# Attention, MLP and routed experts in one kernel: r*k by (d, t) for tiles 3 to 6, lower halves on VectorE, reciprocals by a backward scan

## The chip, the cores and the metric

One core of a Trainium2 chip runs the whole program. The metric is the device time of one execution in microseconds (us). Within the core, TensorE (PE) multiplies matrices out of SBUF into PSUM, VectorE (DVE) and ScalarE (ACT) work elementwise on SBUF and PSUM, GpSimd (POOL) works elementwise on SBUF, and SyncE (SP) issues the DMA transfers. Every engine takes its instructions strictly in the order of its own queue.

## What is computed

Three stages follow one another: a linear attention with a decaying state, an MLP with a leaky activation, and a top-1 mixture of experts.

```python
# attention: B 4, H 8, S 768, D 48
for t in range(S):
    cur = einsum('bhd,bhe->bhde', u[None] * k_t, v_t)
    y[:, :, t] = einsum('bhd,bhde->bhe', r_t, state + cur)
    state = w_t[:, :, :, None] * state + einsum('bhd,bhe->bhde', k_t, v_t)
# MLP: 3072 tokens, 384 -> 2048 -> 384
h = x @ w_in
x = (where(h > 0, h, alpha * h)) @ w_out
# experts: 8 experts, 384 -> 1024 -> 384, one per token
e = argmax(x @ w_gate);  g = softmax(x @ w_gate)[e]
out = g * (relu(x @ w1[e]) @ w2[e])
```

## The kernel before

**Tiles and blocks.** The 3072 tokens are 24 tiles of 128 (`NTILE`); a batch has six (`CPB`), so tiles 0 and 6 begin a sequence (`first`) and tile 5 ends one (`last`). Three tiles make a block of the MLP (`NB`), and there are 8 blocks. The attention of the three tiles of block b+1 is interleaved with the MLP steps of block b. Tiles 0 to 2 have nothing to hide under; they, and the first weights, make up the prologue (slots from `PT0`).

**One attention tile** (`att_tile`). `dm` holds r, k and w with the head dimension on partitions and time along the row, (d, t); `tm` holds r, k and v with time on partitions. `scan` makes the running product of w on DVE (`ex`); POOL multiplies r by it (`decay_r`); `rec` forms its reciprocal on DVE, with one reciprocal of every fourth column (112x128) and three products that fill the columns between (L310); then k is multiplied by the reciprocal (L312). `diag` and `diag_sum` form the diagonal term: POOL multiplies r by k and by u on `tm` (L317, L318), DVE sums over d (`c`, L323), and `diag_v` multiplies v by c on POOL (`cv`). PE makes the scores, ACT copies them out, POOL masks them (`at`, L362), and PE accumulates the output from cv, the state and the masked scores in one bank (`px`). `state` adds the old state to k^T v on DVE and multiplies by the decay `pm` on POOL (L396, L397). `x_out` and `x_low` split the output into a high half on ACT (`xth`) and a low half on DVE (`xtl`, L440).

**Weights.** w_in and w_out come as 64-bit numbers in 16 loads (`wl_dma`, `wl_stages`): per load ACT rescales, DVE does three passes of integer work (L212, L213, L216), ACT rounds the high half, and the low half is one subtraction of 128x768 (L234). The even loads (w_in, `wil`) have it on DVE, the odd ones (w_out, `wol`) on POOL; `LOW_V` says which. Two raw buffers and two `v64` buffers are in use, so a load waits for the words of the one two before it.

**MLP step.** A step is nine matmuls of 128x384 (`p1`), ACT and DVE for the activation (`gn`, then `gt` on DVE), ACT and DVE for its two halves (`gh`, then `gl` on DVE), and, two steps later, nine matmuls of 128x384 (`p2`). After a block, `p2_out` copies three banks of PSUM to `x2`, one of the three on DVE. `gate_block` then routes the block's tokens: in blocks 0 to 5 DVE forms the logits with 24 products that sum (`lv`, L483); in the last two blocks PE does it, with three transposes and three small matmuls per tile (`tr`, `lg`).

**Order.** Slots in a table (`OPS`, `PRO_OPS`, `PRO_MOVED`, times `s_tile`) set where a piece of work is issued. In the prologue all engines keep that order. From the first MLP step on, PE and POOL keep it, and the order on DVE and ACT is chosen by the framework's scheduler.

Of the kernel before, what the change touches and what calls it, by code (L numbers as in the profile page):

```python
# [64 lines left out]
LOW_V = range(0, 16, 2)  # L65
# [6 lines left out]
}  # L72
PT0 = -100
# [28 lines left out]
def attention_mlp_moe(ctx, tc, dmaj, tmaj, ub, alpha, w_in, w_out, w_gate, w_gate_b, wexp, out):  # L102
# [59 lines left out]
    ub_s = cst.tile([128, DM], F32, name="ub_s")  # L162
    al_s = cst.tile([128, NF1], F32, name="al_s")
# [36 lines left out]
    def wl_stages(j):  # L200
# [47 lines left out]

    def constants():
# [20 lines left out]
    def att_tile(i, s0):  # L270
        cx = {}
        blk, j = divmod(i, NB)
        first, last = i % CPB == 0, i % CPB == CPB - 1
# [25 lines left out]
        def rec(n):  # L299
# [5 lines left out]
            if n == 0:  # L305
                vec.reciprocal(out=at4(rc, 3), in_=at4(ex, 3))
            elif n == 1:
                w = dm_t[i][:, 1024:1540].rearrange("p (a t) -> p a t", a=NP)[:, :, 1:129]
                for m in (2, 1, 0):
                    vec.tensor_tensor(out=at4(rc, m), in0=at4(rc, m + 1), in1=at4(w, m + 1), op=ALU.mult)  # L310
            else:
                vec.tensor_tensor(out=cx["k"], in0=cx["k"], in1=rc, op=ALU.mult)  # L312

        def diag():
            tm = tm_t[i]
            rk = ap.tile([128, DM], F32, tag="rk", name="rk", bufs=1)
# [55 lines left out]
        def ktr():  # L372
            pa = ps_a.tile([128, NP, PR], F32, tag="pa", name="pk")
            for p in range(NP):
                pe.transpose(pa[:, p, :], cx["k"][:, p, :], ident[:PR, :PR])
            cx["pk"] = pa

        def ktr_out():
            kt = ap.tile([128, NP, PR], F32, tag="kt", name="kt", bufs=1)
            act.copy(kt, cx["pk"])  # L380
            cx["kt"] = kt

        def kv():
            v = cx["v"]
            pa = y_bank("pv", [PR, NP, 96])
            for p in range(NP):
                pe.matmul(pa[:, p, :], lhsT=cx["kt"][:, p, :], rhs=v[:, 96 * p : 96 * p + 96], start=True, stop=True)
# [49 lines left out]
        def x_low():  # L437
# [5 lines left out]
            "scan": scan, "r": decay_r, "rec0": lambda: rec(0), "rec1": lambda: rec(1), "k": lambda: rec(2),  # L443
            "rk": diag, "c": diag_sum, "cv": diag_v, "sc": scores,
# [3 lines left out]
        if not last:  # L448
            ops.update({"ktr": ktr, "ko": ktr_out, "pm": decay, "kv": kv, "st": state})
        for n, fn in ops.items():  # L450
            if i < NB or (i == NB and n in PRO_NEXT):
                at_slot(PT0 + PRO_MOVED.get((i, n), PTILE * i + PRO_OPS[n]), fn)
            else:
                at_slot(s0 + OPS[n], fn)

    def gate_block(blk, x2, g0):
# [98 lines left out]
        if blk < NBLK - PE_GATES:  # L555
# [545 lines left out]
```

## Time and profile before

| | |
|---|---|
| three runs, median | 864.56 us (861.56 to 866.51) |
| the profiled execution | 865.85 us, of which the span is 864.2 us |
| PE busy | 806.4 us (93%) |
| DVE busy | 639.0 us (74%) |
| ACT busy | 380.1 us (44%) |
| POOL busy | 305.5 us (35%) |
| mean granted TensorE clock | 0.970 |

An engine is busy while one of its instructions executes; an instruction that has begun but is held up counts as busy too, so a long one of a kind that is elsewhere short tells of a hold-up. Idle time in front of an instruction is put down to what ended it (its releaser). The granted clock is 1.00 at 2.4 GHz and 0.50 at 1.2 GHz.

### The profile page before, as it was taken

Reading aid. Unit: us, or ns where it says so; the run is one execution under the profiler, and the core shown is the slowest. Engines: PE = TensorE matmul, PEld = TensorE weight load, DVE = VectorE, ACT = ScalarE, POOL = GpSimd, SP = SyncE. Lnnn points to the kernel's source line nnn. Section 1 sums busy time; section 2 is a strip of 40 time slices with the busy share of each in tenths; the row PEclk is TensorE's granted clock in tenths of the full one; section 3 lists DMA queues with packets and bytes.
Section 4 is the critical chain, followed back from the end, with each engine's and each line's share of the span. In section 5 each row is a group of like instructions: output and inputs, shape, how many; then the busy total and the mean of one; then the engine's idle time right before and its main releaser. Section 6 shows DMA issues by size and latency. Waiting matters only on the chain. (4 is left out here: it accounts for less than half of the span.)

```text
span 864.2 us, 15692 instructions
## 1 busy us (share of the span) xinstructions
PE 806.4 (93%) x5997; PEld 757.0 (88%) x5997; DVE 639.0 (74%) x1195; ACT 380.1 (44%) x727; POOL 305.5 (35%) x338
## 2 busy tenths in 40 slices
PE   5678888999999999999999999999999999999994
PEld 3577768999889989989999989989899999999993
DVE  5999997967967986975986973446776676766761
ACT  1445452344333334333344333346455666565641
POOL 5776625324443234243334331122333122222201
PEclk8889889999999999999999999999999999999998
DMA  9825543022223222322322300155367577686820
GB/s 270 249 89 201 182 146 126 35 66 94 67 66 97 65 66 66 94 66 71 90 66 67 93 1 2 29 201 211 119 229 246 198 235 289 221 286 200 289 104 20
DMA packets 30517, 114.80 MB, mean 133 GB/s; under 512 B 8229, under 2 KB 11592, under 8 KB 30440
## 3 DMA queue, kind: packets, MB, share of 16 engines
q1 hardware_dynamic: 26088, 103.52, 37.5%
q0 software_dynamic: 4352, 10.26, 3.2%
q8 instruction: 48, 0.79, 0.4%
q14 instruction: 29, 0.24, 0.1%
HBM read 104.10 MB, written 10.45 MB: 133 GB/s over the span
## 5 line engine op out<-in xcount | busy, mean ns | idle before, releaser
L582 PE MATMUL ph<-xth,wih 128*128 128x384 f32 x384 | 137.8, 359 | 16.4 <-DVE gt L587 13.5
L582 PE MATMUL ph<-xtl,wih 128*128 128x384 f32 x384 | 131.7, 343 | 7.2 <-DVE xtl L440 7.2
L608 PE MATMUL py<-woh,gh 128*128 128x384 f32 x384 | 135.6, 353 | 2.7 <-DVE x L619 2.4
L582 PE MATMUL ph<-xth,wil 128*128 128x384 f32 x384 | 132.3, 345 | 4.6 <-DVE wil L234 4.6
L593 ACT CAST gh<-gt 128x384 fp32r<-128x384 f32 x128 | 65.7, 513 | 151.0 <-DVE gt L587 150.4
L608 PE MATMUL py<-woh,gl 128*128 128x384 f32 x384 | 129.9, 338 | 0.0
L608 PE MATMUL py<-wol,gh 128*128 128x384 f32 x384 | 129.5, 337 | 0.0
L587 DVE SCALAR_TENSOR_TENSOR gt<-gn,oma_s,ph 128x384 f32<-128x384 f32 x128 | 77.6, 606 | 51.8 <-ACT gn L585 51.6
L595 DVE TENSOR_TENSOR gl<-gt,gh 128x384 fp32r<-128x384 f32 x128 | 87.8, 686 | 28.7 <-ACT gh L593 26.3
L483 DVE SCALAR_TENSOR_TENSOR sink<-x,wgb 128x384 f32<-128x384 f32 x144 | 100.0, 718 | 1.5 <-ACT x L619 1.2
L585 ACT ACTIVATE gn<-ph 128x384 f32<-128x384 f32 x128 | 62.4, 488 | 85.3 <-PE ph L582 82.1
L813 DVE SCALAR_TENSOR_TENSOR gl<-ph,gh 128x256 fp32r<-128x256 f32 x96 | 40.3, 421 | 74.7 <-ACT gh L811 74.4
L582 PEld LDWEIGHTS ph<-xth,wih 128*128 128x128 f32 x384 | 74.0, 193 | 24.1 <-DVE gt L587 16.7
L882 POOL DMA_INDIRECT out<-ys,meta x28 | 28.3, 1012 | 165.2 <-ACT ys L879 109.9
L808 PE MATMUL ph<-xh,w1h 128*128 128x256 f32 x288 | 81.7, 284 | 1.4 <-DVE gl L813 1.3
L608 PEld LDWEIGHTS py<-woh,gh 128*128 128x128 f32 x384 | 73.1, 190 | 9.7 <-issue 3.2
L808 PE MATMUL ph<-xh,w1l 128*128 128x256 f32 x288 | 81.2, 282 | 0.0
L582 PEld LDWEIGHTS ph<-xtl,wih 128*128 128x128 f32 x384 | 74.5, 194 | 7.5 <-DVE xtl L440 7.5
L808 PE MATMUL ph<-xl,w1h 128*128 128x256 f32 x288 | 80.7, 280 | 0.0
L582 PEld LDWEIGHTS ph<-xth,wil 128*128 128x128 f32 x384 | 74.2, 193 | 6.7 <-DVE wil L234 6.7
L362 POOL TENSOR_SCALAR_AFFINE_SELECT at<-at 128x512 f32<-128x512 f32 x46 | 34.2, 764 | 125.6 <-ACT at L358 125.6
L608 PEld LDWEIGHTS py<-woh,gl 128*128 128x128 f32 x384 | 72.8, 190 | 0.6 <-DVE gl L595 0.6
(213 smaller groups left out, 1874.0 us busy)
## 6 DMA issues: line engine op xcount, KB each, us to landing
raw<-w SPq DMA_DIRECT2D x64, 768.0 KB, 4.8
tm<-tmaj SPq DMA_DIRECT2D x21, 704.0 KB, 4.2
dm<-dmaj SPq DMA_DIRECT2D x21, 673.8 KB, 4.8
raw<-w_out SPq DMA_DIRECT2D x8, 768.0 KB, 4.3
raw<-w_in SPq DMA_DIRECT2D x7, 768.0 KB, 5.1
x2d<-x SPq DMA_DIRECT2D x8, 576.0 KB, 4.5
both<-tmaj SPq DMA_DIRECT2D x3, 704.0 KB, 11.1
wgb<-w_gate_b SPq DMA_DIRECT2D x2, 768.0 KB
```

The source lines that it names most:

```text
L362: pool.affine_select(out=cx[jj], in_=cx[jj], pattern=[[0, NP], [1, 128]], compare_op=ALU.is_gt, fill=0.0, base=0, channel_multiplier=-1,)
L483: vec.scalar_tensor_tensor(out=sink, in0=x2[:, j, :], scalar=1.0, in1=wgb_t[h][:, e, :], op0=ALU.mult, op1=ALU.mult, accum_out=cx["l"][:, ...
L582: pe.matmul(ph, lhsT=w, rhs=x[:, c, :], start=k == 0, stop=k == 3 * KC - 1)
L585: act.activation(gn, ph, AF.Relu, scale=-1.0)
L587: vec.scalar_tensor_tensor(out=gt, in0=gn, scalar=oma_s[:, f : f + 1], in1=ph, op0=ALU.mult, op1=ALU.add)
L593: act.copy(gh, gt)
L595: vec.tensor_tensor(out=gl, in0=gt, in1=gh.bitcast(F32), op=ALU.subtract)
L608: pe.matmul(y_t[blk][j], lhsT=g[:, sl], rhs=w, start=f == 0 and m == 0, stop=f == NF1 - 1 and m == 2,)
L808: pe.matmul(ph, lhsT=w, rhs=x, start=k == 0, stop=k == 3 * KC - 1)
L813: vec.scalar_tensor_tensor(out=gl, in0=ph, scalar=0.0, in1=gh.bitcast(F32), op0=ALU.max, op1=ALU.subtract)
L882: pool.indirect_dma_start(out=out, out_offset=bass.IndirectOffsetOnAxis(ap=d["meta"][:, j, 0:1], axis=0), in_=ys, in_offset=None, bounds_c ...
```

## The change

- `NBACK = 7`: for tiles 0 to 6 the reciprocals come from one reciprocal of four columns (112x4, the last of each pair of heads) put into a zeroed tile `inj`, and one scan of 516 columns that runs backward over w. `dm` gets one more column for it (`DMW` 1541 instead of 1540).
- `CPE`, tiles 3 to 6: POOL multiplies r by k in `dm`, once, 112x512; PE forms the sums with u, four matmuls of two columns behind the transposes of k; ACT copies them out with k^T. The second product on POOL and the sum on DVE are gone, the loads of r and k by time are cut away, and `cv` stands three slots later.
- `NSPE = 7`: for tiles 1 to 4 PE adds the old state by one matmul with the identity, and DVE multiplies by the decay out of PSUM. The product on POOL is gone.
- All 16 lower halves of the weights are on DVE.
- The routing of block 0 takes its logits from PE (`0 < blk` in `gate_block`). The constants of the routing are made at slot 34, after block 0, and `1 - alpha` is made on DVE.

```diff
-LOW_V = range(0, 16, 2)
+NSPE = 7
+NBACK = 7
+DMW = 2 * 512 + NP * 129 + 1
+CPE = range(NB, 7)
+OPS_C = {"rk": -10, "cv": 3}
...
-    (3, "scan"): 19.55, (3, "rec0"): 19.58, (3, "rec1"): 21.52, (3, "k"): 21.54,
+    (3, "rk"): 19.5, (3, "scan"): 19.55, (3, "rec0"): 19.58, (3, "rec1"): 21.52, (3, "k"): 21.54,
...
-        sp.dma_start(out=tm, in_=tmaj[i])
+        sl = (slice(None), slice(2 * DM if i in CPE else 0, TMW))
+        sp.dma_start(out=tm[sl], in_=tmaj[i][sl])
...
+    inj = ap.tile([PR, NP, 129], F32, tag="inj", name="inj", bufs=1)
+    pool.memset(inj, 0.0)
...
-            e = vec if j in LOW_V else pool
-            e.tensor_tensor(out=lo, in0=v, in1=hi.bitcast(F32), op=ALU.subtract)
+            vec.tensor_tensor(out=lo, in0=v, in1=hi.bitcast(F32), op=ALU.subtract)
...
-            if n == 0:
+            if n == 0 and i < NBACK:
+                vec.reciprocal(out=inj[:, :, 128], in_=ex[:, :, 127])
+                vec.tensor_tensor_scan(
+                    out=rc.rearrange("p a t -> p (a t)")[:, ::-1],
+                    data0=dm_t[i][:, 1025 : 1025 + NP * 129][:, ::-1],
+                    data1=inj.rearrange("p a t -> p (a t)")[:, ::-1],
+                    initial=0.0,
+                    op0=ALU.mult,
+                    op1=ALU.add,
+                )
...
+            if i in CPE:
+                rk = ap.tile([PR, NP, 128], F32, tag="rk", name="rk", bufs=1)
+                pool.tensor_tensor(out=rk, in0=cx["r"], in1=cx["k"], op=ALU.mult)
+                cx["rk"] = rk
+                return
...
+            if i in CPE:
+                for p in range(NP):
+                    at = NP * PR + 2 * p
+                    pe.matmul(pa[:, at : at + 2], lhsT=cx["rk"][:, p, :], rhs=us_s[:, p, :], start=True, stop=True)
...
+            add = not first and i < NSPE
+            if add:
+                fl = "p a e -> p (a e)"
+                pe.matmul(
+                    pa.rearrange(fl), lhsT=ident[:PR, :PR], rhs=st_t[i - 1].rearrange(fl), start=True, stop=False
+                )
...
-            if first:
+            if first or i < NSPE:
                 vec.tensor_tensor(out=sn, in0=pa, in1=pm, op=ALU.mult)
...
-        if blk < NBLK - PE_GATES:
+        if 0 < blk < NBLK - PE_GATES:
```

The POOL queue in block 0, from the mask of tile 3's scores to the mask of tile 4's. Before (`dm` is r by the decay, `st` the state, `wol` a lower half, `rk` and `cv` the diagonal term):

```order
L362 AFFINE_SELECT at_550<-at_550 128x512
L234 TENSOR_TENSOR wol_123<-v_503,woh_122 128x768
L297 TENSOR_TENSOR dm<-dm,ex 112x512
L397 TENSOR_TENSOR st<-st,pm 112x384
L317 TENSOR_TENSOR rk<-tm 128x384
L318 TENSOR_TENSOR rk<-rk,ub_s 128x384
L234 TENSOR_TENSOR wol_123<-v_594,woh_122 128x768
L234 TENSOR_TENSOR wol_123<-v_718,woh_122 128x768
L330 TENSOR_TENSOR cv<-tm,c 128x256
L330 TENSOR_TENSOR cv<-tm,c 128x128
L362 AFFINE_SELECT at_833<-at_833 128x512
```

The same place after, with the products of tiles 4 and 5 (`rk<-dm`):

```order
L398 AFFINE_SELECT at_539<-at_539 128x512
L349 TENSOR_TENSOR rk<-dm 112x512
L315 TENSOR_TENSOR dm<-dm,ex 112x512
L366 TENSOR_TENSOR cv<-tm,kt 128x256
L366 TENSOR_TENSOR cv<-tm,kt 128x128
L398 AFFINE_SELECT at_823<-at_823 128x512
```

The three lower halves, the state and the product with u have left this stretch; tile 3's cv, which stood ahead of its masks, now stands behind them and behind the two products of tile 4.

The DVE queue where block 0 ends (`c` is the sum of tile 7's diagonal term, COPY is the copy of a finished bank). Before:

```order
L312 TENSOR_TENSOR dm<-dm,rec 112x512
L587 SCALAR_TENSOR_TENSOR gt<-gn,oma_s,ph 128x384
L323 TENSOR_REDUCE c<-rk 128x8
L619 COPY x_1351<-py_601 128x384
L595 TENSOR_TENSOR gl<-gt,gh 128x384
L483 SCALAR_TENSOR_TENSOR sink,lg<-x_1351,wgb 128x384 x4
```

And after:

```order
L342 TENSOR_TENSOR dm<-dm,rec 112x512
L641 SCALAR_TENSOR_TENSOR gt<-gn,oma_s,ph 128x384
L673 COPY x_1345<-py_590 128x384
L649 TENSOR_TENSOR gl<-gt,gh 128x384
L359 TENSOR_REDUCE c<-rk 128x8
```

The copy of the bank now stands ahead of the sum `c`, and the products of the routing that followed are gone from here.

## Rows read from the trace of the kernel before

**Rows 1.** Waits of TensorE, 43.68 to 130 us: total, times, longest (us)
```profile
PE ph L582 <- DVE xtl L440: 7.2, 1, 7.2
PE ph L582 <- DVE gt L587: 6.9, 2, 4.2
PE ph L582 <- DVE wil L234: 4.6, 4, 1.6
```

**Rows 2.** Busy time by stretch, with the granted clock in third place from the end
```profile
26.30:43.70 17.40, 9.95 (x145) 6.99 (x143) 17.13 (x20) 6.92 (x14) 12.45 (x11) 0.89 0.77 239
43.68:130.00 86.32, 70.48 (x474) 61.78 (x475) 84.44 (x105) 43.67 (x80) 50.28 (x41) 0.86 0.47 155
...
146.00:226.00 80.00, 79.76 (x625) 74.46 (x626) 65.45 (x160) 29.36 (x68) 27.59 (x34) 0.98 0.26 78
```

**Rows 3.** DVE in order of time at the end of the prologue: start, duration (us)
```profile
30.54 3.68 DVE L282 TENSOR_TENSOR_SCAN ex<-dm,apat 112x516 f32<-112x516 f32 x1
34.26 0.96 DVE L306 RECIPROCAL rec<-ex 112x128 f32<-112x128 f32 x1
35.13 0.49 DVE L212 TENSOR_SCALAR v<-v 128x768 uint32<-128x768 uint32 x1
...
41.20 1.23 DVE L310 TENSOR_TENSOR rec<-rec,dm 112x128 f32<-112x128 f32 x3
...
43.07 0.55 DVE L440 TENSOR_TENSOR xtl<-px,xth 128x384 fp32r<-128x384 f32 x1
```

**Rows 4.** POOL in order of time beside the scan of rows 3
```profile
29.30 1.73 POOL L397 TENSOR_TENSOR st<-st,pm 112x384 f32<-112x384 f32 x1
30.99 0.98 POOL L330 TENSOR_TENSOR cv<-both,c 128x256 f32<-128x256 f32 x2
31.92 1.23 POOL L362 TENSOR_SCALAR_AFFINE_SELECT at<-at 128x512 f32<-128x512 f32 x2
```

**Rows 5.** Groups of DVE, 43.68 to 130 us: count, busy us, mean ns, idle before
```profile
L595 DVE TENSOR_TENSOR gl<-gt,gh 128x384 fp32r<-128x384 f32 x15 | 12.7, 849 | 0.3 <-ACT gh L593 0.3
...
L212 DVE TENSOR_SCALAR v<-v 128x768 uint32<-128x768 uint32 x14 | 10.2, 726 | 0.3 <-ACT v L208 0.3
...
L234 DVE TENSOR_TENSOR wil<-v,wih 128x768 fp32r<-128x768 f32 x7 | 8.7, 1239 | 0.0
L310 DVE TENSOR_TENSOR rec<-rec,dm 112x128 f32<-112x128 f32 x9 | 6.4, 710 | 0.0
L282 DVE TENSOR_TENSOR_SCAN ex<-dm,apat 112x516 f32<-112x516 f32 x3 | 3.7, 1226 | 0.0
```

**Rows 6.** The lower halves of the whole program: duration ns shortest, median, longest
```profile
L234 DVE TENSOR_TENSOR wil<-v,wih x8: 927/1126/2081, 39.1 to 123.6; 128x768 fp32r<-128x768 f32 x8
```

**Rows 7.** Groups of POOL, 43.68 to 130 us: count, busy us, mean ns, idle before
```profile
L234 POOL TENSOR_TENSOR wol<-v,woh 128x768 fp32r<-128x768 f32 x7 | 19.0, 2714 | 22.7 <-ACT woh L229 22.7
...
L318 POOL TENSOR_TENSOR rk<-rk,ub_s 128x384 f32<-128x384 f32 x2 | 4.9, 2432 | 0.2
L297 POOL TENSOR_TENSOR dm<-dm,ex 112x512 f32<-112x512 f32 x3 | 4.8, 1607 | 0.0
L397 POOL TENSOR_TENSOR st<-st,pm 112x384 f32<-112x384 f32 x3 | 4.0, 1327 | 6.6 <-DVE st L396 6.6
```

**Rows 8.** DVE in order of time where block 0 ends
```profile
145.17 0.55 DVE L323 TENSOR_REDUCE c<-rk 128x8 f32<-128x384 f32 x1 [3.00 <-POOL rk L318]
...
146.10 0.55 DVE L595 TENSOR_TENSOR gl<-gt,gh 128x384 fp32r<-128x384 f32 x1
```

**Rows 9.** TensorE in order of time where block 0 ends
```profile
146.24 0.44 PE L608 MATMUL py<-woh,gh 128*128 128x384 f32 x1 [2.43 <-DVE x L619]
148.03 1.67 PE L387 MATMUL pv<-tm,kt 128*112 128x96 f32 x8
```

**Rows 10.** TensorE in the routing of block 6: transposes and logits of one tile
```profile
543.32 0.49 PE L464 MATMUL px<-ident,x 128*128 128x128 f32 x3
547.15 0.73 PE L472 MATMUL plg<-wg_s,x2t 128*128 128x8 f32 x6
```

More of the change, by code (lines that the diff above doesn't have):

```diff
@@ L247, in attention_mlp_moe, with fill @@
     acc_t = [cst.tile([128, E], BF16, name="acc0")]
+    def fill():
+        vec.tensor_scalar(oma_s, al_s, -1.0, 1.0, op0=ALU.mult, op1=ALU.add)
+        pool.memset(oobm, NT)
+        sp.dma_start(out=metad.rearrange("(p n) c -> p n c", p=128), in_=oobm)
+        sp.dma_start(out=x2d[NT : NT + 1, :].rearrange("o (a t) -> o a t", a=KC), in_=apat[0:1, 0:KC, 1:129])
     def constants():
@@ L272, in att_tile, with inputs @@
         blk, j = divmod(i, NB)
+        def inputs():
+            for n, at in (("r", 0), ("k", 512)):
+                cx[n] = dm_t[i][:, at : at + 512].rearrange("p (a t) -> p a t", a=NP)
         first, last = i % CPB == 0, i % CPB == CPB - 1
@@ L372, in ktr @@
         def ktr():
-            pa = ps_a.tile([128, NP, PR], F32, tag="pa", name="pk")
-            for p in range(NP):
-                pe.transpose(pa[:, p, :], cx["k"][:, p, :], ident[:PR, :PR])
+            pa = ps_a.tile([128, NP * PR + H], F32, tag="pa", name="pk")
+            if not last:
+                for p in range(NP):
+                    pe.transpose(pa[:, PR * p : PR * p + PR], cx["k"][:, p, :], ident[:PR, :PR])
+            if i in CPE:
+                for p in range(NP):
+                    at = NP * PR + 2 * p
+                    pe.matmul(pa[:, at : at + 2], lhsT=cx["rk"][:, p, :], rhs=us_s[:, p, :], start=True, stop=True)
             cx["pk"] = pa
         def ktr_out():
-            kt = ap.tile([128, NP, PR], F32, tag="kt", name="kt", bufs=1)
-            act.copy(kt, cx["pk"])
-            cx["kt"] = kt
+            kt = ap.tile([128, NP * PR + H], F32, tag="kt", name="kt", bufs=1)
+            sl = (slice(None), slice(NP * PR if last else 0, NP * PR + (H if i in CPE else 0)))
+            act.copy(kt[sl], cx["pk"][sl])
+            cx["kt"] = kt[:, : NP * PR].rearrange("p (a d) -> p a d", a=NP)
+            if i in CPE:
+                cx["c"] = kt[:, NP * PR :]
         def kv():
@@ L385, in kv @@
             pa = y_bank("pv", [PR, NP, 96])
+            add = not first and i < NSPE
[4 more added lines that the diff above has]
+                )
             for p in range(NP):
[L387 removed]
+                pe.matmul(
+                    pa[:, p, :], lhsT=cx["kt"][:, p, :], rhs=v[:, 96 * p : 96 * p + 96], start=not add, stop=not add or p == NP - 1
+                )
             cx["pv"] = pa
@@ L448, in att_tile @@
         if not last:
-            ops.update({"ktr": ktr, "ko": ktr_out, "pm": decay, "kv": kv, "st": state})
+            ops.update({"pm": decay, "kv": kv, "st": state})
+        for n in ("c",) if i in CPE else ("ktr", "ko") if last else ():
+            del ops[n]
         for n, fn in ops.items():
@@ L937, in attention_mlp_moe @@
     at_slot(PT0, lambda: sp.dma_start(out=ub_s, in_=ub))
+    at_slot(PT0 + 0.25, lambda: sp.dma_start(out=us_s, in_=ubd))
     at_slot(PT0 + 0.25, lambda: sp.dma_start(out=al_s, in_=alpha))
     at_slot(PT0 + 0.25, lambda: sp.dma_start(out=wg_s, in_=w_gate))
-    at_slot(PT0 + PRO_CONST, constants)
+    at_slot(PT0 + PRO_FILL, fill)
+    at_slot(GATE_CONST, constants)
     for i in range(1, NTILE):
@@ L1075 @@
     ub = np.ascontiguousarray(np.broadcast_to(a["u"].reshape(1, DM), (128, DM)))
+    us = np.zeros((PR, NP, 2), np.float32)
+    for j in range(2):
+        us[64 * j : 64 * j + D, :, j] = a["u"].reshape(NP, 2, D)[:, j].T
     alpha = np.ascontiguousarray(a["moe_alpha"].reshape(NF1, 128).T)
```

44 lines of the change are left out of this document (22 added, 22 removed).

## The prediction

> **What bounds the kernel now.** I read the waits of TensorE first, then busy time by stretch, then the single instructions of VectorE and GpSimd where they are packed. From 146 us on TensorE is busy 79.76 of 80 us at a granted clock of 0.98 [rows 2]: there work of VectorE is free, and each us given to TensorE is a us of the program. Before that it is otherwise. TensorE waits 7.2 us for the last `xtl` of the prologue, and in block 0 for `gt` and `wil`, again VectorE's [rows 1]; it is busy only 70.48 of 86.32 us, so it is idle for 15.8, and its clock is at 0.86, while VectorE is busy 84.44 of the same 86.32 [rows 2]. In the last 17.4 us of the prologue VectorE is busy for 17.13 [rows 2]. So from 26 to about 125 us the program advances as fast as VectorE works through its queue.
>
> Much of that busy time is hold-up. The scan of tile 3 takes 3.68 us from 30.54 on, where the three scans of block 0 take 1.23 each [rows 3, 5]; beside it GpSimd runs the state, a cv and two masks one after another until 33.15 [rows 4], and the scan ends 1.1 us later, about its own length. In block 0, `gl` takes 0.849 on average against 0.55 where GpSimd is still [rows 5, 8], L212 0.726 against 0.49, a product of L310 0.710 against 0.41 [rows 3, 5], `wil` 1.239 against 0.927 [rows 5, 6]. Times their counts: 15 x 0.30 + 14 x 0.24 + 9 x 0.30 + 7 x 0.31 = 12.7 us, on 45 instructions. Some 30 more of the weights and of k read two operands too; at the same 0.28 each they add 8. So VectorE loses an estimated 21 us to 50.28 us of busy GpSimd [rows 2], 0.42 per us.
>
> The Trainium skill says what this is (SBUF — State Buffer, Who interferes with whom): a VectorE instruction with two SBUF inputs and a GpSimd instruction that reads SBUF need the same port, the first holds it to its end and the other stands still. The rows agree: 3.68 beside GpSimd's run, 0.55 for a subtraction alone.
>
> **Block 0, GpSimd's side.** Seven lower halves (19.0 us busy), the second products (4.9) and the states (4.0) leave the stretch [rows 7]. The plain product stays, 512 columns wide and three times instead of twice; at the 1.6 of the decay product, of the same shape, that is at most 2.5 more [rows 7]. Net 25.4 us of 50.28; at 0.42 VectorE gets back 10.7.
>
> **Block 0, VectorE's own work.** Added: seven lower halves at 0.93 [rows 6], 6.5; three backward scans at the forward 1.23 [rows 5], 3.7; three reciprocals of four columns and `oma_s`, at about 0.2 each, 0.8 (one of 128 columns takes 0.96 [rows 3], so between nothing and that). Removed: three reciprocals at 0.96, 2.9, nine products at 0.41, 3.7 [rows 3], three sums at 0.55, 1.6 [rows 8]. Net +2.8. Together -7.9. I take **-6**: each new lower half on VectorE stands behind ScalarE's cast of its high half, with `gt` and `gl` queued behind it, and some of these casts will be late (GpSimd waited 22.7 us for them, harmlessly [rows 7]). Bounds: if the hold-ups do not shrink with GpSimd's work, +2.8; if VectorE gets back all, the 15.8 us of TensorE's idling [rows 2] are the end, and some of it goes on other waits, -12.
>
> The masks, `cv` and the decay stay on GpSimd. cv now stands behind the next tile's two products, some 3.2 us by the same 1.6 [rows 7]; TensorE's `px` needs it two slots, one step, later, and a step of block 0 takes 86.3 / 16 = 5.4 us, so it is covered. If it is not, TensorE stops at `px` with the MLP behind it, 1 to 2 us per tile. TensorE's additions in block 0 (identity matmuls of 384 columns for tiles 3 and 4, no more than the 1.67 that four of 96 took at half clock [rows 9], and the columns for c) lie in its 15.8 idle us: nothing. The identity matmul also makes `kv` wait for the state of the tile before; that is written a third of a block earlier.
>
> **Prologue.** Per tile the reciprocal falls from 0.96 to about 0.2 and the backward scan costs what the three products cost [rows 3]: -0.75. The state and tile 3's second product, 1.73 and about 2.4 [rows 4, 7], leave GpSimd; at 0.42 that is -1.7. For tiles 0 to 2 I count nothing: they wait for loads and for GpSimd's own queue, which loses nothing there but one state. Together **-2.5**, bounds -0.5 (loads and GpSimd set the pace) and -5 (three more tiles gain 0.75 each). Counted at nothing: the memset of `inj`, ahead of work that waits for a load; the small load of u on SP's queue, ahead of tile 3's, whose scan stands behind VectorE's other work; the two stores of the routing's fill, which leave SP earlier than they did; and the routing's constants, a run of short instructions on GpSimd that moves from the middle of block 0 to its end.
>
> **End of block 0.** VectorE sat idle 3.0 us for tile 7's second product on GpSimd [rows 8]; the copy of a bank was queued behind, and TensorE stood 2.43 us for it [rows 9]. The mean clock of the next 80 us is 0.98 [rows 2], that is 3.2 us at 1.2 GHz and 1.6 us lost. Now the copy stands ahead of that sum, and two lower halves and a product are off GpSimd. 2.4 + 1.6 = 4.0; tile 7's sum can still hold up the `gt` behind it, so **-3.5**, bounds 0 and -4.
>
> **Routing of block 0 on TensorE.** Three tiles at 0.49 + 0.73 [rows 10], less what overlaps their neighbours, 2.9; tile 6's c columns, four small matmuls beside the three in that 0.73, 0.6. All of it lies where TensorE is full: **+3.5**, bounds +2.5 and +8 if the transposes wait for banks that the attention of block 1 also uses, as those of block 6 did not have to. The 24 products that VectorE loses there gain nothing.
>
> **Sum.** -2.5 - 6 - 3.5 + 3.5 = -8.5. The profiled execution took 865.85 us (span 864.2 and 1.65 around it): 857.4. It lay 1.3 above the median of 864.56, on which the sum gives 856.1. I say **856.5**. Half a percent, about what a measurement of this kernel can tell from no change, is 4.3 us.
>
> **Rivals.** *The hold-ups stay.* VectorE meets GpSimd's remaining 25 us as often as it met the 50: block 0 +2.8, prologue -1, end of the block -2.5, routing +3.5: 865.85 + 2.8 = 868.7, no change that can be told. For it: GpSimd idles anyway between its bursts [rows 7], and what stays comes in bursts too; against: `gl` shows 0.55 as soon as GpSimd is still [rows 8]. The Trainium skill leans this way (Perfetto Trace Analysis, Optimizing Scalar/DVE Operations): offloading between these two engines may not help, since they share a port. The rows speak against it here: a lower half kept GpSimd busy for 2.71 and takes VectorE 0.93 [rows 6, 7].
>
> *All of it comes back.* Each removed us of GpSimd returns whole, and TensorE's idling caps the gain: 865.85 - 4.5 - 12 - 4 + 3 = 848.4. For it: the scan lost 2.45 us to three instructions [rows 3, 4]; against: `xtl` and the sum, which take an operand from PSUM or have only one, stand at 0.55 [rows 3, 8], so part of VectorE's queue has nothing to get back. The Trainium skill's rule on the port, cited above, would give this result for a queue of two-operand work alone.
>
> *Slower: the backward scan is dear.* No row shows a scan that reads and writes backward. If it takes 3 times the forward 1.23, six of the seven lie on VectorE's chain and cost 6 x 2.46 = 14.8: 872.2. It turns the sign at 8.5 / 6 = 1.4 us each, and passes half a percent at 2.1. Against: products with a stride of four columns took 0.41 for 128, as many per column as the scan's.
>
> *Routing stalls.* Six insertions that wait 1 us each and half clock after them, +6 to +8: 864 to 866.
>
> **How the numbers follow.** Forecast, 852 to 861: 0.54. All given back, below 852: 0.21. Hold-ups stay, or the routing stalls: 0.17. Slower: 0.08. Faster by over 0.5% (below 860.2) takes nearly all of the first two: 0.74; within 0.5%: 0.18; slower: 0.08. The range leaves out the dear scan, the worse half of the unchanged cases and the end of the large gain: 848 to 864.
>
> **What would show it.** In the changed profile: the last `xtl` of the prologue ending near 41 instead of 43.6; block 0's end near 134 instead of 143; VectorE's `gl`, L212 and lower halves near 0.6, 0.55 and 1.0; backward scans at 1.23; no wait of TensorE for a copy at the end of block 0; three transposes and logits there at 1.2 per tile without idle time ahead. Wrong would be: scans over 2 us, TensorE waiting for `cv`, VectorE waiting for `woh`, or TensorE idle in block 1.

## The result, and the profile after

The changed kernel takes 856.01 us (median of 4 runs, 852.84 to 859.88) beside 865.53 us for the kernel before in the same session: a ratio of 0.9897, 95% interval 0.9867 to 0.9928, so 9.5 us less. The profiled execution took 852.84 us with a span of 851.1; it is the shortest of its four, and the pair of profiles is 13.0 us apart.

To see where the time went, each trace is cut at marks that every version has: the start of tile 1's scan (the prologue's loads are there), the end of the third `xtl` (the prologue ends), and the last `p2` matmul of blocks 0, 1 and 2. All in us; "sum" is the four stages from the scan to the end of block 2, where all edits act. The second trace of each kernel is from the experiments.

| trace | to the scan | prologue | block 0 | block 1 | block 2 | sum | what is left of the span |
|---|---|---|---|---|---|---|---|
| before | 13.69 | 29.93 | 97.77 | 69.34 | 66.80 | 263.8 | 586.6 |
| before, again | 12.78 | 29.48 | 95.92 | 69.06 | 66.35 | 260.8 | 586.5 |
| after | 11.65 | 27.78 | 94.50 | 67.83 | 65.55 | 255.7 | 583.8 |
| after, again | 14.29 | 28.87 | 94.73 | 67.82 | 65.56 | 257.0 | 584.5 |

So 8.1 of the first pair's 13 us lie in the stages that the change touches. The other 4.9 are the load ahead of the first scans, which moves by 2.6 us between two executions of the same kernel, and the time behind block 2, where no line of the change acts: over the traces of all versions below it lies between 582.7 and 586.7. The stages alone are 3.8 to 8.1 us shorter, depending on which of the two traces of each kernel are compared.

Busy time in block 0 of the changed kernel (start and end, length, then PE, PEld, DVE, ACT, POOL busy with counts; third from the end the granted clock):

```profile
39.43:134.00 94.57, 82.35 (x587) 74.64 (x587) 86.04 (x119) 50.64 (x93) 34.58 (x33) 0.91 0.46 152
```

Beside [rows 2], whose stretch ends 11 us before block 0 does: TensorE's clock is now 0.91 instead of 0.86 (0.87 over the whole of block 0 before), and VectorE is no longer busy for all but 2 us of the stretch: it idles 8.5 us. TensorE is still idle for 12.2 us there, and its waits say for whom (changed kernel, 39 to 138 us: total, times, longest):

```profile
PE px L461 <- POOL cv L366: 4.6, 4, 2.1
PE ph L636 <- DVE gt L641: 3.8, 1, 3.8
PE ph L636 <- DVE wil L246: 2.7, 2, 1.5
PE ph L636 <- ACT wih L242: 1.1, 1, 1.1
```

The 7.2 us for `xtl` and nearly half of what [rows 1] had for `gt` and `wil` are gone. The first line is new. The groups of VectorE between 39.43 and 125 us (count, busy us, mean ns, idle before):

```profile
L649 DVE TENSOR_TENSOR gl<-gt,gh 128x384 fp32r<-128x384 f32 x15 | 11.0, 731 | 0.0
L641 DVE SCALAR_TENSOR_TENSOR gt<-gn,oma_s,ph 128x384 f32<-128x384 f32 x16 | 9.7, 608 | 2.0 <-ACT gn L639 1.9
L225 DVE TENSOR_SCALAR v<-v 128x768 uint32<-128x768 uint32 x14 | 8.8, 630 | 1.0 <-ACT v L221 1.0
L246 DVE TENSOR_TENSOR wol<-v,woh 128x768 fp32r<-128x768 f32 x8 | 8.2, 1022 | 0.2 <-ACT woh L242 0.2
L246 DVE TENSOR_TENSOR wil<-v,wih 128x768 fp32r<-128x768 f32 x7 | 6.6, 943 | 0.4 <-ACT wih L242 0.4
...
L492 DVE TENSOR_TENSOR xtl<-px,xth 128x384 fp32r<-128x384 f32 x4 | 2.2, 550 | 2.3 <-ACT xth L487 2.3
```

Against [rows 5], `gl` fell from 849 to 731 ns, the word pass (L212, now L225) from 726 to 630, `wil` from 1239 to 943; `wol` is new here at 1022. The idle time is in front of `gt`, `xtl` and the word pass. VectorE now waits for ScalarE: ahead of `gt` and `xtl` for what ScalarE reads from TensorE, ahead of the word pass for its rescaling of the weights.

VectorE in order of time at the end of the prologue and where block 0 ends:

```profile
28.68 1.22 DVE L302 TENSOR_TENSOR_SCAN ex<-dm,apat 112x516 f32<-112x516 f32 x1
29.93 0.18 DVE L324 RECIPROCAL inj<-ex 112x4 f32<-112x4 f32 x1
30.15 2.83 DVE L325 TENSOR_TENSOR_SCAN rec<-dm,inj 112x516 f32<-112x516 f32 x1
...
133.78 0.56 DVE L673 COPY x<-py 128x384 f32<-128x384 f32 x1 [1.15 <-PE py L662]
...
136.54 0.55 DVE L359 TENSOR_REDUCE c<-rk 128x8 f32<-128x384 f32 x1 [0.91 <-POOL rk L354]
```

The forward scan of tile 3 is back at 1.22 (3.68 in [rows 3]); the backward one now meets GpSimd and takes 2.83. At the end of the block the copy stands ahead of the sum and waits for TensorE; in [rows 8, 9] TensorE waited for it.

### The profile page after: what moved, and what is told of

It is laid out like the page before. It is cut to its first block, busy times and chain, and to the rows that moved or that the text cites. A ratio compares the mean times of both kernels' runs of the same rounds, so it can differ in the third digit from the quotient of the medians.

```text
span 851.1 us, 15767 instructions
## 1 busy us (share of the span) xinstructions
PE 808.6 (95%) x6064; PEld 760.3 (89%) x6064; DVE 612.0 (72%) x1141; ACT 382.9 (45%) x731; POOL 283.7 (33%) x322
## 5 line engine op out<-in xcount | busy, mean ns | idle before, releaser
L636 PE MATMUL ph<-xth,wih 128*128 128x384 f32 x384 | 135.5, 353 | 10.6 <-DVE gt L641 9.5
L636 PE MATMUL ph<-xth,wil 128*128 128x384 f32 x384 | 130.0, 339 | 2.7 <-DVE wil L246 2.7
L636 PE MATMUL ph<-xtl,wih 128*128 128x384 f32 x384 | 129.7, 338 | 0.0
L649 DVE TENSOR_TENSOR gl<-gt,gh 128x384 fp32r<-128x384 f32 x128 | 86.7, 678 | 30.9 <-ACT gh L647 28.6
L639 ACT ACTIVATE gn<-ph 128x384 f32<-128x384 f32 x128 | 62.5, 489 | 94.5 <-PE ph L636 91.4
L398 POOL TENSOR_SCALAR_AFFINE_SELECT at<-at 128x512 f32<-128x512 f32 x46 | 40.4, 896 | 156.5 <-ACT at L394 153.4
L636 PEld LDWEIGHTS ph<-xth,wih 128*128 128x128 f32 x384 | 72.9, 190 | 16.6 <-DVE gt L641 11.4
L537 DVE SCALAR_TENSOR_TENSOR sink<-x,wgb 128x384 f32<-128x384 f32 x120 | 82.9, 714 | 1.5 <-ACT x L673 1.2
L862 PE MATMUL ph<-xh,w1h 128*128 128x256 f32 x288 | 81.3, 282 | 1.1 <-DVE gl L867 0.9
```

What stands on the lines that cost most here:

```text
L398: pool.affine_select(out=cx[jj], in_=cx[jj], pattern=[[0, NP], [1, 128]], compare_op=ALU.is_gt, fill=0.0, base=0, channel_multiplier=-1,)
L537: vec.scalar_tensor_tensor(out=sink, in0=x2[:, j, :], scalar=1.0, in1=wgb_t[h][:, e, :], op0=ALU.mult, op1=ALU.mult, accum_out=cx["l"][:, ...
L636: pe.matmul(ph, lhsT=w, rhs=x[:, c, :], start=k == 0, stop=k == 3 * KC - 1)
L639: act.activation(gn, ph, AF.Relu, scale=-1.0)
L649: vec.tensor_tensor(out=gl, in0=gt, in1=gh.bitcast(F32), op=ALU.subtract)
L862: pe.matmul(ph, lhsT=w, rhs=x, start=k == 0, stop=k == 3 * KC - 1)
```

## The experiments

How much VectorE is held up is worked out over all the traces together: in the stretch of block 0 from the third to the sixth `xtl`, each instruction gets the shortest spacing that its kind shows over all the traces (the lower eighth), and what it takes beyond that is "lost"; cut a little otherwise, the figures move by up to 0.6. GpSimd's busy time in the same stretch counts what holds GpSimd up too, so beside it stands its work alone, each instruction at the shortest duration of its kind (again the lower eighth). All in us.

| kernel | stretch | work alone | lost | idle | GpSimd busy | GpSimd's work alone |
|---|---|---|---|---|---|---|
| before | 86.7 | 66.2 | 19.3 | 1.7 | 50.3 | 36.4 |
| before + lower halves on VectorE (lowdve) | 85.9 | 73.0 | 9.6 | 3.6 | 38.6 | 26.1 |
| after | 83.6 | 69.1 | 9.5 | 5.8 | 31.0 | 18.8 |
| after, odd lower halves on GpSimd (lowpool) | 90.6 | 62.8 | 18.8 | 9.0 | 45.7 | 33.7 |
| after without CPE (nocpe) | 81.3 | 71.6 | 8.5 | 1.8 | 43.0 | 19.9 |
| after without CPE, halves on GpSimd (nocpe_lowpool) | 86.0 | 64.2 | 16.4 | 5.1 | 46.8 | 31.6 |
| after without NSPE (nospe) | 84.5 | 68.7 | 11.4 | 4.8 | 31.1 | 22.7 |
| after, products of the next tile behind cv (cvfirst) | 80.7 | 69.1 | 8.3 | 4.1 | 28.8 | 18.8 |

And the times, with the stages:

| kernel | median us (runs) | ratio to before, 95% | prologue | block 0 | block 1 | block 2 | sum |
|---|---|---|---|---|---|---|---|
| again_before | 864.15 (10) | 0.9986, 0.9962 to 1.0009 | 29.48 | 95.92 | 69.06 | 66.35 | 260.8 |
| again_after | 856.00 (4) | 0.9870, 0.9824 to 0.9917 | 28.87 | 94.73 | 67.82 | 65.56 | 257.0 |
| lowdve | 860.42 (10) | 0.9946, 0.9922 to 0.9970 | 29.05 | 94.70 | 66.86 | 66.80 | 257.4 |
| lowpool | 865.35 (10) | 0.9997, 0.9973 to 1.0021 | 27.09 | 102.73 | 67.83 | 65.53 | 263.2 |
| gatedve | 849.61 (4) | 0.9817, 0.9783 to 0.9852 | 27.93 | 93.25 | 65.04 | 66.19 | 252.4 |
| cvfirst | 854.66 (4) | 0.9894, 0.9851 to 0.9936 | 27.99 | 91.40 | 67.82 | 65.57 | 252.8 |
| nocpe | 852.17 (4) | 0.9846, 0.9807 to 0.9885 | 27.63 | 89.00 | 69.84 | 65.57 | 252.0 |
| noback | 855.94 (4) | 0.9882, 0.9836 to 0.9927 | 30.21 | 94.53 | 67.85 | 65.57 | 258.2 |
| nocpe_lowpool | 858.96 (6) | 0.9930, 0.9903 to 0.9957 | 26.58 | 96.81 | 74.12 | 65.55 | 263.1 |
| nospe | 858.56 (10) | 0.9925, 0.9902 to 0.9947 | 27.99 | 95.94 | 67.83 | 65.55 | 257.3 |
| nocpe_gatedve | 851.18 (4) | 0.9850, 0.9808 to 0.9892 | 25.42 | 91.85 | 66.42 | 66.83 | 250.5 |
| cpe6_gatedve | 849.52 (4) | 0.9834, 0.9794 to 0.9875 | 25.93 | 90.49 | 65.52 | 66.14 | 248.1 |

The intervals are 2 to 4 us to either side, so of single steps of 2 us only the stages speak. Of gatedve all four runs (up to 850.74) lie below all eight of the changed kernel (from 852.84); nocpe's four (849.26 to 853.37) just overlap with them.

**The two kernels again (again_before, again_after).**

> The kernel before, unchanged, profiled once more. Stages are read in the trace: the prologue from the start of tile 1's scan to the end of the last xtl (29.9 us in the first profile), block 0 from there to the start of its last p2 matmul (97.8), block 1 from there to its own last p2 matmul (69.3), and the rest (653.4 to the end of the span). If stages are steady from run to run, each comes back within 1 us and tile 1's scan starts near 13.7. If the start of the loads and the later blocks vary, the scan may start up to 2 us elsewhere and the rest may differ by 2 to 4 us; then the changed kernel's 2.0 us earlier scan and its 4.1 us shorter rest are no work of the change.

> The changed kernel, unchanged, profiled once more. Its first profile is 13.0 us faster than that of the kernel before, its median 9.5. If 13.0 is the change's own, the time is near 853 again, with prologue 27.8, block 0 94.5, block 1 67.8 and the rest 649.4. If 4 to 6 us of it are variation of the loads' start and of blocks that no line of the change touches, the time is near 857, the three stages stay within 1 us, and the rest goes back to 652 to 654.

They give the ground on which the rest stands: 8.2 us apart by medians, 3.8 by the stages of these two traces (8.1 by those of the first pair). Blocks 1 and 2 repeat within 0.5 us, block 0 within 1.9 and the prologue within 1.1.

**The lower halves alone, on the kernel before (lowdve).**

```diff
-LOW_V = range(0, 16, 2)
+LOW_V = range(0, 16)
```

> The kernel before with one part of the change alone: all lower halves on VectorE. Theory of the prediction (hold-ups shrink with GpSimd's work, 0.42 us per us): VectorE takes 7 x 0.93 = 6.5 us more in block 0 and gets back 0.42 x 19.0 = 8.0: block 0 at 96, the time 1 to 2 us below that of the kernel before. Rival (hold-ups stay): block 0 at 104, the time 6 us above. Rival (all comes back): GpSimd's 12.7 us alone come back whole, block 0 at 91 to 92, the time 6 us below.

Groups of VectorE, 41 to 130 us:

```profile
L595 DVE TENSOR_TENSOR gl<-gt,gh 128x384 fp32r<-128x384 f32 x16 | 11.6, 724 | 0.3 <-ACT gh L593 0.3
...
L234 DVE TENSOR_TENSOR wol<-v,woh 128x768 fp32r<-128x768 f32 x8 | 8.4, 1049 | 1.2 <-ACT woh L229 1.2
L234 DVE TENSOR_TENSOR wil<-v,wih 128x768 fp32r<-128x768 f32 x7 | 6.9, 981 | 0.2 <-ACT wih L229 0.2
```

This one line halves the hold-ups: 9.6 us lost instead of 19.3, `gl` at 724, which is all that the whole change reached (731). The hold-ups that stay are not those of the lower halves. What VectorE gets back it pays with the halves themselves, 73.0 instead of 66.2, so the stretch from tile to tile shrinks little (85.9; 85.9 in the second trace of before); block 1 is 2.2 to 2.5 us shorter and the median 3.7 to 4.6 lower.

**The lower halves back on GpSimd (lowpool), and the same without CPE (nocpe_lowpool).**

```diff
-            vec.tensor_tensor(out=lo, in0=v, in1=hi.bitcast(F32), op=ALU.subtract)
+            (pool if j % 2 else vec).tensor_tensor(out=lo, in0=v, in1=hi.bitcast(F32), op=ALU.subtract)
```

> The changed kernel with this part alone undone: the odd lower halves on GpSimd again. Theory: block 0 1 to 2 us longer than the changed kernel's 94.5, and more if the masks and cv, which TensorE now waits for, stand behind the lower halves on GpSimd's queue: waits of TensorE for cv and masks, 4.6 us in the changed kernel's block 0, then grow to 6 or more. Rival (hold-ups stay): block 0 at 88, the time 6 us below the changed kernel's. Rival (all comes back): block 0 at 100.

Lowpool's waits of TensorE, 39 to 142 us, and the longest of them in its GpSimd's order of time:

```profile
PE px L461 <- POOL cv L366: 15.0, 4, 7.8
...
110.82 3.28 POOL L246 TENSOR_TENSOR wol<-v,woh 128x768 fp32r<-128x768 f32 x1 [8.95 <-ACT kt L422]
114.07 2.25 POOL L398 TENSOR_SCALAR_AFFINE_SELECT at<-at 128x512 f32<-128x512 f32 x2
116.29 1.26 POOL L349 TENSOR_TENSOR rk<-dm 112x512 f32<-112x512 f32 x1
117.63 3.02 POOL L315 TENSOR_TENSOR dm<-dm,ex 112x512 f32<-112x512 f32 x1
120.61 2.00 POOL L366 TENSOR_TENSOR cv<-tm,kt 128x256 f32<-128x256 f32 x2
```

Without this part nothing of the gain is left: 865.35, block 0 at 102.73. The hold-ups are back (18.8), and TensorE stops 15.0 us for `cv`, which stands at the end of a queue of five. My reading then was that the lower halves are worth more here than in lowdve because cv stands behind them; nocpe_lowpool, where cv stands further ahead, tests that.

> The changed kernel with two parts undone: the diagonal term of tiles 3 to 6 as before, and the odd lower halves on GpSimd. Undone alone, the lower halves cost the changed kernel 8.1 us of block 0, and TensorE then waited 15 us for cv. Theory (that loss is GpSimd's queue: cv stands behind masks, products and lower halves, and with cv ahead of them again the lower halves are worth what they were worth in the kernel before): block 0 at 91 to 92, 2 to 3 us above the 89.0 with the diagonal term alone undone, the time 854 to 856. Rival (a lower half on VectorE is worth more as such, by the hold-ups): block 0 at 97, the time near 860.

That reading fell. TensorE waits for no cv in nocpe_lowpool, and yet block 0 takes 96.8 (89.0 in nocpe) and the median is 858.96 against 852.17. The waits are VectorE's and ScalarE's (`gt` 6.7, `wil` 4.0, `wih` 3.9 us), and the copy at the end of block 0 costs 3.1 again. Why the lower halves are worth 4 us in the kernel before, and 7 to 9 in the changed one, stays open.

**CPE undone (nocpe), and cv moved up (cvfirst).** In the changed kernel the GpSimd and TensorE in order of time about tiles 4 and 5:

```profile
50.06 4.33 POOL L398 TENSOR_SCALAR_AFFINE_SELECT at<-at 128x512 f32<-128x512 f32 x2 [12.61 <-ACT at L394]
54.35 2.08 POOL L349 TENSOR_TENSOR rk<-dm 112x512 f32<-112x512 f32 x1
56.51 1.38 POOL L315 TENSOR_TENSOR dm<-dm,ex 112x512 f32<-112x512 f32 x1
57.85 2.00 POOL L366 TENSOR_TENSOR cv<-tm,kt 128x256 f32<-128x256 f32 x2
78.58 1.69 POOL L349 TENSOR_TENSOR rk<-dm 112x512 f32<-112x512 f32 x1 [18.73 <-PE pk L416]
80.23 3.93 POOL L398 TENSOR_SCALAR_AFFINE_SELECT at<-at 128x512 f32<-128x512 f32 x2
84.14 3.79 POOL L315 TENSOR_TENSOR dm<-dm,ex 112x512 f32<-112x512 f32 x1
87.89 2.40 POOL L366 TENSOR_TENSOR cv<-tm,kt 128x256 f32<-128x256 f32 x2
```

```profile
58.83 0.69 PE L461 MATMUL px<-ident,cv 128*128 128x128 f32 x2 [2.10 <-POOL cv L366]
```

Two things delay cv: the two products ahead of it, and, at 78.58, a wait of the first product for `pk` of TensorE. Its tile has one buffer, so the product of tile 5 waits until TensorE has read tile 4's; masks and cv are queued behind it. Two buffers for it were not tried.

```diff
-OPS_C = {"rk": -10, "cv": 3}
+OPS_C = {"rk": -7, "r": -7, "cv": 3}
```

> The changed kernel with the next tile's products r*k and r*decay moved on GpSimd's queue behind the present tile's cv (slot -7 instead of -10 and -9). In the changed kernel TensorE waits 4.6 us for cv in block 0, which the prediction had called covered. If that wait is on the path: no wait for cv, block 0 at 91 to 92 instead of 94.6, the time 3 to 4 us below the changed kernel's 856. Rival: VectorE's pace sets block 0, and the waits for gt, wil and wih grow from 7.6 us by as much as the wait for cv falls: block 0 at 94 to 95, the time unchanged.

The waits of cvfirst's TensorE, 39 to 142 us:

```profile
PE ph L636 <- DVE wil L246: 4.4, 3, 2.5
PE ph L636 <- DVE gt L641: 3.8, 1, 3.8
PE ph L636 <- ACT wih L242: 2.4, 2, 1.3
```

The wait for cv is gone and block 0 is 3.1 to 3.3 us shorter. Other waits took back part of the 4.6 us: those for `wil` and `wih` grew from 3.8 to 6.8, and TensorE's idle time in block 0 fell from 12.2 to 10.7 only, so the rest of the gain lies in its busy time (80.8 instead of 82.3 to 82.5). The median moved by 1.3 only, which its interval does not tell from 3 or from nothing.

```diff
-CPE = range(NB, 7)
+CPE = range(0)
...
-    (3, "rk"): 19.5, (3, "scan"): 19.55, ...
+    (3, "scan"): 19.55, ...
```

> The changed kernel with the diagonal term of tiles 3 to 6 as before: two products of GpSimd on the tile by time, the sum on VectorE, cv ahead of the masks. Theory (hold-ups at 0.42): GpSimd does 1.0 us alone more per tile, busy 2.4, and VectorE 0.55: 3 x (0.55 + 1.0) = 4.7 us more for VectorE in block 0, but the 4.6 us of waiting for cv are gone: block 0 between 94 and 98. Block 1 is longer by up to 2.4 if VectorE again waits for a second product ahead of the bank's copy. The time 857 to 862. Rival (r*k by (d, t) is worth nothing, as its gain goes into the wait for cv): block 0 at 92 to 94, the time 853 to 856.

Nocpe's waits of TensorE, 40 to 142 us:

```profile
PE ph L636 <- DVE gt L641: 5.2, 1, 5.2
PE ph L636 <- DVE wil L246: 4.2, 4, 2.0
PE ph L636 <- ACT wih L242: 2.6, 2, 1.8
PE py L662 <- DVE x L673: 1.7, 1, 1.7
```

Its block 0 by busy time, and the matmuls that the change adds to block 0 of the changed kernel (39.43 to 133.93 us: the sums with u, then the identity; count, busy us, mean ns, idle before):

```profile
40.65:129.65 89.00, 76.72 (x554) 68.65 (x555) 86.97 (x121) 49.40 (x92) 48.76 (x36) 0.94 0.50 167
```

```profile
L416 PE MATMUL pk<-us_s,rk 112*128 112x2 f32 x32 | 3.8, 242 | 0.0
L433 PE MATMUL pv<-st,ident 112*112 112x384 f32 x4 | 1.6, 484 | 0.0
```

With the two products, the sum on VectorE and its 2.5 us of work back, block 0 takes 89.0 instead of 94.5. The copy's wait returns (1.7), and block 1 takes 2.0 more. By the medians the kernel is 3.8 us faster without CPE, by the stages 3.7 to 5.0. TensorE's idle time in block 0 is not what falls: it is 12.3 us, as in the changed kernel (12.2), because waits for `gt`, `wil` and `wih` take the place of those for cv. Its busy time falls, from 82.3 to 76.7. The small matmuls of the sums with u are gone from it, 3.8 us busy, of which some overlap with their neighbours. The clock makes about 3 us, an estimate: 8.9 us of TensorE's busy time in block 0 lie at 1.2 GHz instead of 14.7 (mean clock 0.94 instead of 0.91). GpSimd is busy 12 us more (43.0), and VectorE loses 8.5, no more than in the changed kernel; but what came on top is GpSimd held up itself, for its work alone is only 1.1 us more. Its `cv`, 40.10 to 121.30 us, shows it; in the kernel before a `cv` took 1125 ns on average:

```profile
L366 POOL TENSOR_TENSOR cv<-tm,c 128x256 f32<-128x256 f32 (+1 forms) x6 | 15.3, 2570 | 23.8 <-DVE c L359 21.2 <-PE px L461 2.6
```

**The routing of block 0 back on VectorE (gatedve).**

```diff
-        if 0 < blk < NBLK - PE_GATES:
+        if blk < NBLK - PE_GATES:
```

> The changed kernel with the routing of block 0 back on VectorE (24 products instead of TensorE's transposes and logits). Theory of the prediction: TensorE is full in block 1, so the move cost 2.9 us there and the freed VectorE gained nothing: block 1 at 65 instead of the changed kernel's 67.8, the time 2 to 3 us below the changed kernel's 856. Rival: VectorE's 24 products hold up gt and gl of block 1 and the start of block 2, so undoing brings back waits of TensorE: block 1 and 2 together not shorter than 133.4, the time the same or above.

In the changed kernel the routing stands on TensorE like this (the first rows of each kind for three tiles; between them stand the MLP and the attention, and none shows a wait):

```profile
137.99 0.49 PE L518 MATMUL px<-ident,x 128*128 128x128 f32 x3
...
143.55 0.83 PE L526 MATMUL plg<-wg_s,x2t 128*128 128x8 f32 x6
```

Without it, block 1 is 2.8 us shorter and block 2 0.6 longer. The median fell by 6.4, the stages by 3.3 (4.6 beside the second trace of after). Not explained are 1.2 of these in block 0, where nothing differs until the block's end, and what the median has beyond the stages; behind block 2 the traces differ by 1.1 to 1.8 us.

**Backward scan and states undone (noback, nospe).**

```diff
-NBACK = 7
+NBACK = 0
```

> The changed kernel with the reciprocals of tiles 0 to 6 as before (one reciprocal of 128 columns and three products instead of four columns and the backward scan). Theory: VectorE takes 0.96 - 0.18 = 0.78 us more per tile, the products as long as the scan: prologue 29.1 instead of 28.3 (one tile on the chain, the others behind loads and GpSimd), block 0 up by 2.3 to 97, the time 3 us above the changed kernel's 856. Rival: GpSimd's queue sets both, prologue and block 0 within 0.5 us of the changed kernel, the time unchanged.

```diff
-NSPE = 7
+NSPE = 0
```

> The changed kernel with the state of tiles 1 to 4 as before: sum on VectorE, product with the decay on GpSimd, no matmul with the identity. Theory (0.42 us per us of GpSimd): three states in block 0 at 1.3 busy are 1.7 us, tile 1's in the prologue 0.7: block 0 at 96, prologue at 28.5 to 29, the time 858. Rival (GpSimd's state stands behind cv and holds up the next tile's products, cv comes later): waits for cv above 6 us, block 0 at 98. Rival (the identity matmul costs TensorE what it saves): block 0 at 94 to 95, the time 856.

In noback the reciprocal of tile 3 takes 0.96 us again and the three products 1.23, as in [rows 3]. Its prologue is 1.3 to 2.4 us longer than in the two traces of after, block 0 the same; the median does not show it. Without the states on TensorE VectorE loses 11.4 instead of 9.5, block 0 is 1.2 to 1.4 longer and the median 2.6 higher.

**Two versions put together (nocpe_gatedve, cpe6_gatedve).** The first joins the two edits; the second keeps CPE for tile 6 alone, whose sums relieve the end of block 0.

```diff
-CPE = range(NB, 7)
+CPE = range(6, 7)
```

> The changed kernel with the two parts undone that cost it time when undone alone: the diagonal term of tiles 3 to 6 as before (gain 3.8 us against the changed kernel's median) and the routing of block 0 on VectorE (gain 6.4). If they lie in different stretches, they add: block 0 at 89, block 1 at 65 plus the 1.7 us in which the copy of a bank stands behind tile 7's sum, the time near 846. If the copy's wait and VectorE's 24 products meet, block 1 is at 68 and the time 849.

> As the run with both parts undone, but tile 6 alone keeps its diagonal term by (d, t), so that GpSimd has two products less ahead of tile 7's sum where block 0 ends. If that sum is what holds up the bank's copy: block 0 at 89 to 90, no wait of TensorE for a copy, block 1 at 65 to 66, the time 1 to 2 us below that run's, near 845. If tile 6's cv, later on GpSimd's queue, makes TensorE wait instead, the time is not below it.

Waits of cpe6_gatedve's TensorE, 39 to 142 us:

```profile
PE ph L636 <- DVE gt L641: 6.5, 1, 6.5
PE ph L636 <- DVE wil L246: 3.4, 4, 1.6
PE ph L636 <- ACT wih L242: 3.1, 3, 2.2
PE py L662 <- DVE x L673: 0.2, 1, 0.2
```

By the medians the gains do not add up: nocpe_gatedve gives 851.18, no better than either edit. By the stages most of them do: its sum is 250.5, 5.2 below that of after, where the two edits alone are 3.7 and 3.3 below. Its block 0 takes 91.85 instead of nocpe's 89.0, but its prologue is 2.2 shorter; both stages together are 117.3 and 116.6. Block 1 takes 1.4 and block 2 0.6 more than in gatedve. In cpe6_gatedve the copy's wait is 0.2, cv's is gone, and its stages have the smallest sum of all, 248.1. By the median (849.52) it stands level with gatedve (849.61): these two beat both kernels, the changed one by 6.4 us.

## Why the prediction was right, and where its steps were not

The forecast of 856.5 lies 0.5 us from the median, and the sum of -8.5 beside -8.1 by the stages of the first pair. The second pair gives -3.8, so that the sum comes this close to one pair is in part luck. Its terms missed in opposite directions: block 0 gave 2.7 less than its step said, blocks 1 and 2 together 2.8 more than theirs.

**Prologue, -2.5: about right.** -2.2 in the first pair, -0.6 in the second. The mechanism stands: with the old reciprocal it is 1.3 to 2.4 longer. The last `xtl` ended at 39.4, not 41, because the first scans began 2.0 us earlier in this execution, which is not the change's. But the larger part of the term, 1.7 us for the work that leaves GpSimd, does not show: the prologue is 27.99 with the states back on GpSimd (nospe) and 27.63 with tile 3's products back (nocpe), beside 27.78 and 28.87 in the traces of after. What the backward scan gives is more than the 0.75 counted for it.

**The scan is not dear.** Backward scans took 1.22 and 1.23 us where GpSimd was idle or began after them (5.28, 45.88 and 118.59 us) and 2.10 to 3.13 where it did not; that rival falls by the rows (shortest, median, longest in ns, first and last start in us):

```profile
L325 DVE TENSOR_TENSOR_SCAN rec<-dm,inj x4: 1220/1672/2835, 30.1 to 118.6; 112x516 f32<-112x516 f32 x4
L325 DVE TENSOR_TENSOR_SCAN rec<-both,inj x3: 1234/2097/3133, 5.3 to 19.6; 112x516 f32<-112x516 f32 x3
```

**Block 0, -6: half of it came.** -3.3 in the first pair, -1.2 in the second. The VectorE parts were well sized: 9.8 us of hold-up returned (10.7 forecast), 2.9 of work were added (2.8 forecast). The step that failed is "so it is covered" for `cv`. The prediction named the wait and its price if the cover was gone, 1 to 2 us per tile; it measured 4.6 in all, cvfirst took away that wait and made block 0 3.1 to 3.3 us shorter, and VectorE idled 4.1 us more than before, where 1.9 had been discounted for late casts. I had compared cv's delay with a step of the MLP and not followed what the first product itself waits for, TensorE's use of the tile's only buffer.

A second step failed beside it: TensorE's additions "lie in its 15.8 idle us: nothing". They are 5.4 us busy in block 0, 3.8 for the sums with u and 1.6 for the identity (tile 6's sums, priced at 0.6 in the routing's term, stand in block 0 too), and the idle time fell only from 15.9 to 12.2. Nocpe shows that the sums with u are not hidden: without them, and with cv ahead of the masks again, the idle time stays at 12.3 and the busy time falls by 5.6. So CPE was counted as a gain, and costs some 4 us: what it saves is small, 1.1 us of GpSimd's work alone and 2.5 of VectorE's, and TensorE pays for what it adds, the matmuls and a later cv.

**The rate of 0.42 us per busy us of GpSimd does not hold.** With the lower halves on GpSimd VectorE loses 16.4 to 19.3 us, without them 8.3 to 11.4, and the busy time does not follow: 43.0 us of it go with 8.5 lost (nocpe), 45.7 with 18.8 (lowpool). The error lies in the base. Busy time counts GpSimd's own hold-ups, as the 2432 ns of the second product in [rows 7] do, a kind whose shortest in that trace is 992. Against GpSimd's work alone the loss rises in most versions: 8.3 to 9.5 at 19 to 20 us, 11.4 at 22.7, 16.4 to 18.8 at 32 to 34, 19.3 at 36.4, an estimate of 0.6 us per us from the ends of this row. Lowdve does not fit, 9.6 at 26.1. By it seven halves cost 9.7 us, 1.4 each, and by nospe three states 1.9; of the second products CPE takes away too little work to tell (9.5 lost with CPE, 8.5 without). Whether the kind of instruction counts beside the amount is not shown.

The product with the rate came out by luck: GpSimd's busy time fell by 19.3 us and not by the 25.4 of the step, because what stayed became longer, and 9.8 came back. Nor is it only instructions with two operands in SBUF that lost time, as the step has it: the word pass L212 reads one, and fell from 726 to 630 ns too. The rival that all comes back would have left nothing lost, and 9.5 remain; the one that the hold-ups stay is refuted by 19.3 to 9.5.

The Trainium skill (Perfetto Trace Analysis, Optimizing Scalar/DVE Operations) had spoken for that rival: moving work between these two engines might not help. Here it did in this direction, by 4 us alone and 7 to 9 in the changed kernel, and it pays back what the work itself takes: 6.8 us of VectorE's time for 9.7 of hold-up.

**End of block 0, -3.5: right.** TensorE has no wait for the copy. Block 1 fell by 1.5 with the routing in it; without the routing (gatedve) it is 65.0, 4.0 to 4.3 below before. More than half of that, 2.2 to 2.5, comes with the lower halves alone (lowdve, where the copy's wait is 1.2). The 1.6 counted for the clock are seen in one trace of before (block 1 at 0.975); in the other the clock is 1.00 there and the wait 3.0. Nocpe shows what the wait hangs on: with the diagonal terms as before, tile 7's sum, which waits for its second product, again stands ahead of the copy, and TensorE waits 1.7 us.

```profile
132.73 0.55 DVE L359 TENSOR_REDUCE c<-rk 128x8 f32<-128x384 f32 x1 [3.22 <-POOL rk L354]
```

**Routing on TensorE, +3.5: right in sign, a little large.** Block 1 pays 2.8 and block 2 gets 0.6 back, where I had counted the 24 products at nothing. No transposes waited for banks.

**Left out: block 2.** It became 0.8 to 1.3 us shorter. About half of that is the routing's products off VectorE: with them back (gatedve) it is 0.6 longer. The wait for `gt` near 243 us is still there (1.1 us before, 0.9 at 232.6 after); of the two that the first trace of before has, the one at 227.7 (0.7) is gone, but it is not in the second trace of before either.

Open are the worth of the lower halves in the one kernel and the other, whether they hold VectorE up more than other work of GpSimd, why the two best edits do not add by the medians, and gatedve's part outside block 1.

## What to carry to other kernels

When instructions of two engines hold each other up, both look busy: size what a move frees by the shortest duration of each kind, not by busy time, and undo the parts of the change one at a time; a rate per busy microsecond gives a sum that may come out, and then credits parts that cost. Of a result that gets further work put ahead of it in a queue, follow the whole chain to the engine that needs it, with every buffer that has a single copy. Work given to an engine that idles is not free for that: here the idle time stayed and the busy time grew. And a change of several parts that comes out as forecast is still worth taking apart: here one part was needed for all of the gain, and two, undone each alone, gave 4 and 6 us more.

## What was not expected of the hardware

GpSimd's remaining instructions became longer as those of VectorE shown above became shorter: its products with the running product of w took 2185 ns on average in the changed block 0 (1607 in [rows 7]):

```profile
L398 POOL TENSOR_SCALAR_AFFINE_SELECT at<-at 128x512 f32<-128x512 f32 x6 | 10.7, 1790 | 28.1 <-ACT at L394 25.0 <-ACT kt L422 3.1
L315 POOL TENSOR_TENSOR dm<-dm,ex 112x512 f32<-112x512 f32 x3 | 6.6, 2185 | 0.2
```

The masks took 1790 here, a mean of 896 over the whole program. In block 0 TensorE waits for cv, which stands behind them, and never for the masks. That either of the two is held is what the Trainium skill's rule would give (SBUF — State Buffer, Who interferes with whom: the one that issues first holds the shared pair). Rows of the changed kernel agree. The forward scan of tile 3 begins at 28.68 and takes its usual 1.22 us; GpSimd's product, which begins 0.16 later, takes 2.12, and 1.26 elsewhere (lowpool, at 116.29). At 19.43 it is the other way round:

```profile
19.43 1.18 POOL L315 TENSOR_TENSOR both<-both,ex 112x512 f32<-112x512 f32 x1 [2.23 <-DVE ex L302]
19.61 2.10 DVE L325 TENSOR_TENSOR_SCAN rec<-both,inj 112x516 f32<-112x516 f32 x1
...
28.84 2.12 POOL L349 TENSOR_TENSOR rk<-dm 112x512 f32<-112x512 f32 x1 [1.36 <-DVE c L359]
```

How the turns fall where both queues are packed is not worked out here. The second surprise is that the start of tile 1's scan, which waits for a load, moves between 11.65 and 14.29 us from one execution to another of the same kernel: of a pair of profiles 2 to 3 us are not the change's.
